# q and k of pairs 4 to 31 loaded by casting transfers of GpSimd, and two more pairs' P turned by TensorE

## The chip, the cores and the metric

The kernel runs on one core of a Trainium2 chip. The metric is the device time of one execution in microseconds (us). TensorE is called PE here, VectorE DVE, ScalarE ACT, GpSimd POOL and SyncE SP; SP only issues transfers.

## The reference

Attention with a forgetting gate, for 8 batches of 8 heads, 576 positions and 64 columns a head, and behind it a gated feed-forward block over the 4608 rows that come out.

```python
scores = (q @ k.T) / sqrt(64)                     # per head, 576 x 576
cum    = cumsum(log(clip(f, 1e-4, 1)), axis=-1)
scores = where(causal, -1e9, scores + cum[..., :, None] - cum[..., None, :])
attn   = exp(scores - max);  attn = attn / (sum(attn) + 1e-9)
x      = (attn @ v) as [4608, 512]                # the heads side by side
g      = x @ w_gate                               # [4608, 1536]
out    = (g * sigmoid(g) * (x @ w_val)) @ w_out   # [4608, 512]
```

## The kernel before

Two neighbouring heads are a *pair*; there are 32 pairs, four to a batch. A pair's query rows are 9 blocks of 64, and the blocks fall into two groups, g = 0 (blocks 0 to 3) and g = 1 (blocks 4 to 8). For each pair the work is:

- **Loads** (`load_pair`). k and q come as fp32, two heads at a time, k in 96 partitions of 6 rows and q in 72 partitions of 8 rows. For pairs 4 to 31 SP issues them into the buffers `kf` and `qf`, two of each. `cb`, the cumulated gate, is loaded with them. Pairs 0 to 3 are loaded in parts (`load_parts`), by SP and ACT.
- **Preparation** (`prepare`, `prepare_parts`). k and q are cast to bf16 (`kb`, `qb`, two buffers each), q with the factor -1/8; for pairs 4 to 31 POOL does this. PE then turns them, by transposes of 64 columns of one head each (`turned`), into the PSUM tile `tx`, and ACT or DVE copies the result to `kt` and `qz` in SBUF, where q's two heads stand in a layout with zeros between them.
- **Scores** (`scores`). PE multiplies `qz` with `kt` into the PSUM tiles `sp`. DVE (L652) subtracts the sum from the gate and takes the row's minimum, and ACT (L672) takes the exponential with the row's sum, into `e` and `eo`.
- **Normalisation** (`normalize`). DVE takes the reciprocals (L690) and POOL scales the rows to bf16 (`pk`, L708). This is the matrix P, in 6 blocks of 128 columns for g = 0 and 19 for g = 1. P has to be turned: for the pairs in `ON_PE` (0 to 7) by PE, a block in two transposes, through PSUM, with evacuations by ACT or DVE (L743); from `JFROM` = 8 on by one transposing DMA of SP for both groups (L721).
- **P times v** (`weighted`, `spread`). PE multiplies, and ACT or DVE writes the result into `xT`, a ring of 2048 rows.

The feed-forward block goes over tiles of 256 or 512 rows of that ring: `gate` multiplies with `wg` and `wv` (PSUM tiles `gv`, L201), ACT takes a tanh, DVE multiplies twice, and `project` multiplies with `wo` and stores. The weights come in pieces by casting transfers of POOL (`weights`, L824 and L828).

All of this is written as a list of operations with allowed engines, estimated costs and priorities. The class `Plan` places them on the engines before the program is made, each at the earliest time by its own estimates, and this fixes each engine's order of instructions. `STARTUP` gives the order of the first loads, `HEAD` that of the first groups of scores, and `NUDGE` small changes of priority for each unit of work (q12: the preparation of pair 12; a12.0: its attention, group 0; f and o: the feed-forward block; v: v's casts). `SLACK` is how long a waiting owner of a shared PSUM pool keeps others out. The engines run their lists in order, and a wait holds up everything behind it on its engine.

Of the kernel before, what the change touches and what calls it, by code (L numbers as in the profile page):

```python
# [8 lines left out]
F32 = mybir.dt.float32  # L9
# [198 lines left out]


def mm(*cols):  # L210
    return sum(max(29, c / 2.4 + 2.5) for c in cols)
# [3 lines left out]
def kernel(  # L215
# [42 lines left out]

    ON_PE = {(p, g) for p in range(8) for g in range(2)}

    JFROM = 8
    TWO = False
    NDIRECT = 0

# [11 lines left out]
    FREE = 8  # L276
    SLACK = 400
    SOON = 8
    BACK = 4
    CBACK = 5  # L280
    STARTUP = "p0 q1 f9 v01 k0 p2 wv2 q0 v04 wv0 wg2 wg0 k2 v00 c3 c1 q3 q2 wv4 v02 p4 c2 v03 c4 wg4 v11 c5 wv8 wg8 v10 v14 p5 v13 wo4 p6 v12 c6 wo0 c7 p7 wo8 c0"
    HEAD = "00 10 20 30 11 01 31 21"


    NUDGE = "a0.0:-6 a1.0:-12.5 a10.0:1 a10.1:1.5 a12.0:-0.5 a13.0:0.5 a13.1:-1 a15.0:-1 a15.1:1 a16.0:-3 a17.0:-2 a17.1:-1.5 a18.0:-0.5 a21.0:-1 a21.1:-1 a22.1:0.5 a25.1:-1 a26.1:-1.5 a27.0:-1.5 a27.1:1 a29.0:2 a30.1:-1 a31.0:0.5 a31.1:0.5 a4.0:2.5 a4.1:2.5 a5.0:-1.5 a5.1:-1 a6.0:0.5 a6.1:1 a7.1:-0.5 a8.0:-1 a9.1:-0.5 f0:4 f1:2 f11:-4 f3:-5 f4:-3.5 f5:-4 f6:-2 f7:1 f8:9.5 f9:0.5 o0:-1 o1:-991 o10:-12.5 o11:3.5 o4:1 o5:-7 o6:-4.5 o8:1 o9:9 q0:-8.5 q1:-12 q10:-1.5 q11:-3 q12:-1.5 q13:-3 q14:-4 q15:-2 q16:-6 q17:1.5 q18:-4 q19:-2 q2:-10 q21:0.5 q24:0.5 q26:2.5 q27:0.5 q29:-2 q3:-9.5 q30:-4 q4:-7 q5:-5 q6:-1 q8:-1 v1:-5.5 v2:-2 v3:3.5 v4:1.5 v5:5.5 v6:0.5 v7:-5"

# [154 lines left out]
    def half(key):  # L441
        return pl.buf(key).bitcast(BF16)


    def load_pair(p):
        b, hp = divmod(p, NPB)
        s = first[p]
        if p < NHALF:
            load_parts(p)
            return  # L450
        for name, src, pr in (("k", k, 0), ("q", q, .1)):
            pl.key((name + "f", p), name + "f")
            loads[name, p] = pl.op({"SP": 620} if p else {"ACT": 620}, lambda e, name=name, src=src: (nc.scalar if e == "ACT" else nc.sync).dma_start(
                out=pl.buf((name + "f", p))[0:ROWS[name][0], :, :],
                in_=src[b, 2 * hp:2 * hp + 2].rearrange("h (p r) d -> p h (r d)", r=ROWS[name][1])),
                (), [(name + "f", p)], (-99 + 3 * p if p < NPB else s - SOON) + pr, dma=1060, pk=68 if name == "k" else 86, after=[sums[p - BACK, 0 if p - BACK >= NPB else 1]] if p >= NPB else [])
        if p >= NSEL:
            pl.key(("cb", p), "cb", p)
            for h in range(2):
                loads["cb", p, h] = pl.op({"SP": 600}, lambda e, h=h: nc.sync.dma_start(  # L460
                    out=pl.buf(("cb", p))[64 * h:64 * h + 64, :],
                    in_=cum_dram[2 * p + h:2 * p + h + 1, :].to_broadcast((64, S))),
                    ["cum_dram"], [("cb", p), (("cb", p), 3)], -98.5 + 3 * p if p < NPB else s - SOON + .2, dma=570, pk=93, after=[sums[p - CBACK, 0 if p - CBACK >= NPB else 1]] if p >= NPB + 1 else [])

    def prepare(p):
# [4 lines left out]
        for name in ("k", "q"):  # L470
            fk, bk = (name + "f", p), (name + "b", p)
            KR, KC = ROWS[name]
            pl.key(bk, name + "b")

            def cast(e, name=name, fk=fk, bk=bk, KR=KR):
                src = pl.buf(fk)[0:KR, :, :].rearrange("p h (r d) -> p r h d", d=D)
                dst = pl.buf(bk)[0:KR, :, :, :]
                if e == "ACT":
                    nc.scalar.activation(dst, src, AF.Copy, scale=-scale if name == "q" else 1.0)
                elif name == "q":  # L480
                    eng[e].tensor_scalar(dst, src, -scale, 1.0, op0=ALU.mult, op1=ALU.mult)  # L481
                else:
                    eng[e].tensor_copy(dst, src)
            engs = {"POOL": 850 if p < 8 else 800 if name == "k" else 1010}
            if p < NPB:
                engs = {"POOL": 850, "ACT": 850, "DVE": 500} if name == "k" else {"POOL": 1050, "ACT": 1050, "DVE": 680}
            o = pl.op(engs, cast, [fk], [bk], s - 1 + (name == "q") * .1)
            o.bias = SPARE if p else {}
            tk = ("tt", name, p)
# [4 lines left out]
            def transpose(e, bk=bk, tk=tk, KR=KR, KC=KC):  # L494
                src = pl.buf(bk).rearrange("p r h d -> p r (h d)")
                for j in range(KC):
                    turned(nc, half(tk)[:, KR * j:KR * j + KR], src[0:KR, j, :], ident[0:KR, 0:KR])
            pl.op({"PE": KC * (KR / 2.4 + 2.5)}, transpose, [bk], [tk, ok], s - 1, lat=200)
            halves = [(0, P, None)] if name == "k" else [(0, 64, 0), (64, 128, 1)]
            for a, z, h in halves:  # L500
                def evac(e, a=a, z=z, h=h, tk=tk, ok=ok, KC=KC):
                    if h is None:
                        src = half(tk)[a:z, 0:S].rearrange("r (j p) -> r p j", j=KC)
                        dst = pl.buf(ok)[a:z, :].rearrange("r (p j) -> r p j", j=KC)
                    else:
                        src = half(tk)[a:z, 0:S].rearrange("r (j i p) -> r i j p", j=R, i=NB)
                        dst = pl.buf(ok)[a:z, :, h, :].rearrange("r i (j p) -> r i j p", j=R)
                    if e == "ACT":
                        nc.scalar.copy(dst, src)  # L509
                    else:  # L510
                        nc.vector.tensor_copy(dst, src)
# [11 lines left out]
    def load_parts(p):  # L523
        b, hp = divmod(p, NPB)
        pl.key(("cb", p), "cb", p)
        for name, x, a, z, r, n in parts(p):
            fk = (name + "f", p, x)
            pl.key(fk, name + "f")
            m = (z - a) // r

            def load(e, u, fk=fk, src=(k if name == "k" else q), a=a, z=z, r=r, m=m):
                h0 = 2 * (hp + u)
                (nc.scalar if e == "ACT" else nc.sync).dma_start(  # L533
                    out=pl.buf(fk)[m * u:m * u + m, :, 0:r * D],
                    in_=src[b, h0:h0 + 2, a:z].rearrange("h (p r) d -> p h (r d)", r=r))
# [12 lines left out]
    def prepare_parts(p):  # L548
        for name, x, a, z, r, n in parts(p):
            fk, bk, tk = (name + "f", p, x), (name + "b", p, x), ("tt", name, p, x)  # L550
            m = (z - a) // r
            pr = min(at[p + u, x == "B"] for u in range(n)) - 1 + (name == "q") * .1
            pl.key(bk, name + "b")
            pl.key(tk, "tx", line="q")

            def cast(e, name=name, fk=fk, bk=bk, r=r, w=m * n):
                src = pl.buf(fk)[0:w, :, 0:r * D].rearrange("p h (r d) -> p r h d", d=D)
                dst = pl.buf(bk)[0:w, 0:r, :, :]
                if e == "ACT":
# [13 lines left out]
            def transpose(e, bk=bk, tk=tk, r=r, w=m * n):  # L573
                src = pl.buf(bk).rearrange("p r h d -> p r (h d)")
                for j in range(r):
                    turned(nc, half(tk)[:, w * j:w * j + w], src[0:w, j, :], ident[0:w, 0:w])
            pl.op({"PE": r * (m * n / 2.4 + 2.5)}, transpose, [bk], [tk] + (oks if x == "A" else []), pr, lat=200, holds=oks)
# [239 lines left out]
    def weights():  # L817
        def piece(engs, fn, reads, writes, *a, **kw):
            loads[writes[0]] = pl.op(engs, fn, reads, writes, *a, **kw)

        cuts = [0, 256, 512, 1024, 1536]
        for a, z in zip(cuts, cuts[1:]):
            for nm, wt, src in (("wg", wg, moe_w_gate), ("wv", wv, moe_w_val)):
                piece({"POOL": 600}, lambda e, wt=wt, src=src, a=a, z=z: nc.gpsimd.dma_start(  # L824
                    out=wt[:, :, a:z], in_=src[:, a:z].rearrange("(ko p) n -> p ko n", p=P)),
                    (), [(nm, n) for n in range(a // P, z // P)], 2 + a / 256, dma=5.1 * (z - a) + 880, pk=20 if z - a == 256 else 42)
        for c in range(0, KF, 4):
# [120 lines left out]
    def unit(o):  # L948
        w = o.writes[0] if isinstance(o.writes[0], tuple) else (o.writes[0],)
        n, *i = w[0] + w[1:] if isinstance(w[0], tuple) else w  # L950
        if n in ("kb", "qb", "kt", "qz", "cm", "kf", "qf", "cb") or n == "tt" and isinstance(i[0], str):
            return f"q{i[0] if n != 'tt' else i[1]}"
# [52 lines left out]
```

## Time and profile before

| | |
|---|---|
| time, median of 3 runs | 414.56 us (410.96, 414.56, 416.29) |
| the profiled execution's own time | 415.21 us |
| its span, in which the profile sees instructions | 413.4 us |
| granted clock of PE in it | 1.0 |
| PE busy | 392.5 us (95%) |
| DVE, ACT, POOL busy | 333.2, 320.5, 271.1 us |
| moved by DMA | 72.16 MB, mean 175 GB/s |

A row of a group names the line, the engine, the operation, what it writes and reads, and how often; behind the bar stand the busy time in us and the mean of one in ns; behind the next bar the engine's idle time before these instructions, and what ended it. A row of the waits reads: engine, tile and line that waited, what it waited for, us in total, times, longest. A row of the timeline starts with the start in us and the length.

### The profile page before, as it was taken

To read this page: it belongs to the slowest core of one execution; us is meant where nothing else is said; L and a number is where in the kernel's file an instruction comes from. 1 tells how busy PE (TensorE), PEld (TensorE's weight loads), DVE (VectorE), ACT (ScalarE), POOL (GpSimd) and SP (SyncE) were. 2 spreads that over 40 slices of the span, in tenths; PEclk is the share of its full clock that TensorE was granted. 3 is DMA by queue.
4 is the path that set the end of the run, shared out by engine and by line. 5 is a ranking of instruction groups with operands and counts; after the bars stand their busy time and mean duration, and the time that the engine had idled before them with its cause. 6 is when DMAs were issued, how large, how long until landed. Compare 5 with 4: busy or idle time off the path is not lost.

```text
span 413.4 us, 15350 instructions
## 1 busy us (share of the span) xinstructions
PE 392.5 (95%) x5848; PEld 269.3 (65%) x5848; DVE 333.2 (81%) x1270; ACT 320.5 (78%) x904; POOL 271.1 (66%) x475
## 2 busy tenths in 40 slices
PE   3988988889999999999999999999999999999996
PEld 2667878777666765567776666665566555568775
DVE  4799987798999789999998999899989952775232
ACT  5799988799999998979998897998899653332221
POOL 7679966699996887799789798878777340000000
PEclk9999999999999999999999999999999999999999
DMA  7999979879799999999999999978996744000211
GB/s 192 190 216 226 216 126 247 163 189 210 184 230 191 229 196 233 241 203 230 224 196 223 234 210 225 239 215 182 201 223 114 149 93 126 2 2 28 79 53 52
DMA packets 144026, 72.16 MB, mean 175 GB/s; under 512 B 117904, under 2 KB 131728, under 8 KB 143952
## 3 DMA queue, kind: packets, MB, share of 16 engines
q1 hardware_dynamic: 137856, 66.21, 74.4%
q0 software_dynamic: 5808, 4.72, 7.9%
q8 instruction: 45, 0.74, 0.8%
q14 instruction: 29, 0.24, 0.2%
q10 hardware_dynamic: 288, 0.26, 0.2%
HBM read 46.65 MB, written 9.58 MB: 136 GB/s over the span
## 4 chain that ended last, share of the span: by engine, by line
PE 81%; DMA 6%; DVE 5%; ACT 3%; issue 2%; POOL 1%; SPq 1%; POOLq 0%; ACTq 0%
PE gv L201 63%; PE sp L201 9%; PE tx L764 4%; PE tx L207 3%; DMA wg<-in_moe_w_gate_dram 3%; DVE t L652 3%; DMA kf<-in_k_dram 2%; PE gv L207 2%; DMA vf<-in_v_dram 1%; ACT eo L672 1%; ACT e L672 1%; SPq L533 1%; POOL vt L811 0%; DVE th L857 0%; ACT kt L509 0%
## 5 line engine op out<-in xcount | busy, mean ns | idle before, releaser
L652 DVE CUSTOM_DVE_ANT_0 t<-sp,cb 128x320 f32<-128x320 f32 (+7 forms) x272 | 121.7, 463 | 9.7 <-PE sp L201 5.1
L708 POOL TENSOR_SCALAR pk<-e,lr 128x512 bf16<-128x512 f32 (+3 forms) x189 | 101.5, 541 | 41.9 <-DVE lr L690 19.7
L201 PE MATMUL gv<-xT,wg 128*64 128x512 bf16 (+2 forms) x1152 | 112.7, 326 | 2.5 <-issue 1.4
L201 PE MATMUL gv<-xT,wv 128*64 128x512 bf16 (+2 forms) x1152 | 112.4, 326 | 0.1
L201 PE MATMUL gv<-wo,hh 128*64 128x512 bf16 (+1 forms) x888 | 106.5, 373 | 0.0
L857 DVE SCALAR_TENSOR_TENSOR th<-th,gv 128x512 f32<-128x512 f32 x108 | 73.9, 684 | 31.3 <-ACT th L855 30.5
L672 ACT ACTIVATE e<-t,tm 128x448 f32<-128x448 f32 (+4 forms) x160 | 88.9, 557 | 5.1 <-DVE tm L652 4.7
L855 ACT ACTIVATE th<-gv 128x512 f32<-128x512 f32 x108 | 64.3, 595 | 35.8 <-PE gv L201 35.2
L201 PE MATMUL sp<-kt,qz 128*64 128x512 bf16 (+7 forms) x640 | 77.9, 294 | 5.3 <-DVE tm L652 3.4
L708 POOL TENSOR_SCALAR pk<-eo,lr 128x256 bf16<-128x256 f32 (+3 forms) x128 | 70.4, 550 | 12.3 <-DVE lr L690 9.0
L201 PEld LDWEIGHTS <-wg 128*64 128x64 bf16 x1152 | 58.8, 110 | 30.0 <-issue 1.6
L201 PEld LDWEIGHTS <-wv 128*64 128x64 bf16 x1152 | 59.8, 110 | 27.4 <-issue 0.4
L860 DVE TENSOR_TENSOR hh<-th,gv 128x512 bf16<-128x512 f32 x108 | 73.7, 684 | 4.8 <-PE gv L201 1.8
L672 ACT ACTIVATE eo<-t,tm 128x256 f32<-128x256 f32 (+3 forms) x128 | 71.3, 558 | 4.3 <-DVE tm L652 3.1
L201 PEld LDWEIGHTS <-hh 128*64 128x64 bf16 x888 | 50.7, 110 | 31.3
L201 PEld LDWEIGHTS <-qz 128*64 128x64 bf16 x640 | 41.7, 113 | 23.0 <-issue 5.9
L884 ACT ACTIVATE ot<-gv 128x512 f32<-128x512 f32 (+1 forms) x34 | 19.9, 584 | 26.2 <-PE gv L201 26.0
L652 DVE DVE_READ_ACCUMULATOR2_ANT tm<- 128x1 f32 x432 | 35.7, 83 | 0.0
L652 DVE CUSTOM_DVE_ANT_0 t<-sp,cm,tm 128x64 f32<-128x64 f32 x128 | 34.4, 277 | 1.2 <-PE sp L201 0.3
L481 POOL TENSOR_SCALAR qb<-qf 72x1024 bf16<-72x1024 f32 x28 | 29.2, 1045 | 2.7 <-DMA qf<-in_q_dram 2.6
L672 ACT ACTIVATION_READ_ACCUMULATOR e<-t,tm 128x1 f32 x160 | 30.8, 193 | 0.0
L764 PE MATMUL tx<-pT,vt 128*64 128x320 bf16 (+4 forms) x448 | 29.6, 263 | 1.2 <-ACT pT L743 0.7
(73 smaller groups left out, 432.3 us busy)
## 6 DMA issues: line engine op xcount, KB each, us to landing
out_dram<-ot SPq DMA_DIRECT2D x35, 256.0 KB
vf<-in_v_dram SPq DMA_DIRECT2D x32, 256.0 KB
cb<-cum_f SPq DMA_DIRECT2D x56, 144.0 KB
kf<-in_k_dram SPq DMA_DIRECT2D x28, 288.0 KB
qf<-in_q_dram SPq DMA_DIRECT2D x28, 288.0 KB
wo<-in_moe_w_out_dram POOLq DMA_DIRECT2D x3, 512.0 KB, 7.0
vf<-in_v_dram SPq DMA_DIRECT2D x8, 128.0 KB
wv<-in_moe_w_val_dram POOLq DMA_DIRECT2D x2, 512.0 KB, 8.8
```

The lines of the kernel that those rows point to most:

```text
L201: nc.tensor.matmul(out[c, :], lhsT[:, c], rhs, **kw)
L207: nc.tensor.transpose(out[c, :], src[:, c], ident)
L481: eng[e].tensor_scalar(dst, src, -scale, 1.0, op0=ALU.mult, op1=ALU.mult)
L533: (nc.scalar if e == "ACT" else nc.sync).dma_start(out=pl.buf(fk)[m * u:m * u + m, :, 0:r * D], in_=src[b, h0:h0 + 2, a:z].rearrange("h (p ...
L652: nc.vector.tensor_tensor_reduce(out=pl.buf(tk)[:, a:z], in0=pl.buf(sk)[:, o:o + z - a], in1=pl.buf(("cm", p))[:, i, :] if own else pl.buf ...
L672: nc.scalar.activation(pl.buf(ek)[:, :L], pl.buf(tk)[:, :L], AF.Exp, bias=pl.buf(("tm", p, g))[:, 0, i:i + 1], scale=-1.0, accum_out=pl.bu ...
L708: eng[e].tensor_scalar(dst, src, r, 1.0, op0=ALU.mult, op1=ALU.mult)
L764: nc.tensor.matmul(xo[r, 0:QB * n], vt[:, c, 2 * hp + h, :], pT[:, a:a + n, 64 * h:64 * h + 64], start=(c == 0), stop=(c == nch - 1))
L855: pl.op({"ACT": 487}, lambda e, u=u: nc.scalar.activation(pl.buf(("th", t, u)), pl.buf(("wg", t, u)), AF.Tanh, scale=0.5), [("wg", t, u)], ...
L857: pl.op({"DVE": 605}, lambda e, u=u: nc.vector.scalar_tensor_tensor(pl.buf(("th", t, u)), pl.buf(("th", t, u)), 1.0, pl.buf(("wg", t, u)), ...
L860: pl.op({"DVE": 605}, lambda e, u=u: nc.vector.tensor_mul(pl.buf(("hh", t, u)), pl.buf(("th", t, u)), pl.buf(("wv", t, u))), [("u", t, u), ...
L884: nc.scalar.mul(pl.buf(ok)[:, a:z], pl.buf(bk)[:, 0:z - a], 0.5)
```

## The change

For pairs 4 to 31, POOL issues the loads of q and k as transfers that cast from fp32 to bf16, straight into `qb` and `kb`, of which there are now three each (`NQB`). The casts of these pairs by POOL and the buffers `qf` are gone, `kf` is left for pairs 0 to 3, whose bf16 rows now have buffers of their own (`kc`, `qc`) and whose q comes by way of a `cm` buffer. The two heads of a row stand one behind the other in the bf16 buffers instead of side by side, which `turned_rows` takes into account; number and shape of the transposes stay. The factor -1/8 of q moves from the cast into the evacuation of `qz`. `ON_PE` takes in pairs 8 and 9, and `JFROM` is 10. The rule that keeps casting transfers of POOL apart at the start now holds for weights alone (`o.dma > 1100`). `SLACK`, `STARTUP` and `NUDGE` are new, so the whole order of the instructions is. By the instruction lists, two of the 16 additions of the mask (`cm`, L607) go from POOL to DVE.

```diff
+def turned_rows(nc, out, src, ident):
+    for h in range(2):
+        nc.tensor.transpose(out[64 * h:64 * h + 64, :], src[:, h, :], ident)
...
-    ON_PE = {(p, g) for p in range(8) for g in range(2)}
-    JFROM = 8
+    ON_PE = {(p, g) for p in range(10) for g in range(2)}
+    JFROM = 10
+    NQB = 3
...
-    SLACK = 400
+    SLACK = 100
-    STARTUP = "p0 q1 f9 v01 k0 p2 wv2 q0 v04 wv0 wg2 wg0 k2 v00 c3 c1 q3 q2 wv4 v02 p4 c2 v03 c4 wg4 v11 c5 wv8 wg8 ..."
+    STARTUP = "f9 p0 q1 k0 v01 p2 wv2 q0 wg2 v04 wv0 v00 wg0 q3 c1 c3 k2 wv4 p4 q2 v02 c2 c4 wg4 v03 wg8 v11 wv8 c0 p5 ..."
-    NUDGE = "a0.0:-6 a1.0:-12.5 a10.0:1 ..."
+    NUDGE = "a0.0:0.5 a0.1:-3 a1.0:-85.5 ..."
...
-    bufs("qf", [P, 2, ROWS["q"][1] * D], F32, 2)
-    bufs("kf", [P, 2, ROWS["k"][1] * D], F32, 2)
-    bufs("qb", [P, ROWS["q"][1], 2, D], BF16, 2)
-    bufs("kb", [P, ROWS["k"][1], 2, D], BF16, 2)
+    bufs("kf", [P, 2, 5 * D], F32, 2)
+    bufs("qc", [P, 2, 4 * D], BF16, 2)
+    bufs("kc", [P, 2, 5 * D], BF16, 2)
+    bufs("qb", [P, 2, ROWS["q"][1] * D], BF16, NQB)
+    bufs("kb", [P, 2, ROWS["k"][1] * D], BF16, NQB)
...
-            loads[name, p] = pl.op({"SP": 620} if p else {"ACT": 620}, lambda e, name=name, src=src: (nc.scalar if e == "ACT" else nc.sync).dma_start(
-                out=pl.buf((name + "f", p))[0:ROWS[name][0], :, :],
-                in_=src[b, 2 * hp:2 * hp + 2].rearrange("h (p r) d -> p h (r d)", r=ROWS[name][1])),
+            loads[name, p] = pl.op({"POOL": 560}, lambda e, src=src, bk=bk, w=ROWS[name]: nc.gpsimd.dma_start(
+                out=pl.buf(bk)[0:w[0], :, :], in_=src[b, 2 * hp:2 * hp + 2].rearrange("h (p r) d -> p h (r d)", r=w[1])),
...
-            def cast(e, name=name, fk=fk, bk=bk, KR=KR):
-                ...
-            engs = {"POOL": 850 if p < 8 else 800 if name == "k" else 1010}
-            ...
-            o = pl.op(engs, cast, [fk], [bk], s - 1 + (name == "q") * .1)
...
-                src = pl.buf(bk).rearrange("p r h d -> p r (h d)")
                 for j in range(KC):
-                    turned(nc, half(tk)[:, KR * j:KR * j + KR], src[0:KR, j, :], ident[0:KR, 0:KR])
+                    turned_rows(nc, half(tk)[:, KR * j:KR * j + KR], pl.buf(bk)[0:KR, :, D * j:D * j + D], ident[0:KR, 0:KR])
...
-                    if e == "ACT":
+                    if h is not None and e == "ACT":
+                        nc.scalar.mul(dst, src, -scale)
+                    elif h is not None:
+                        nc.vector.tensor_scalar(dst, src, -scale, None, op0=ALU.mult)
+                    elif e == "ACT":
                         nc.scalar.copy(dst, src)
...
-        if "POOL" in o.engs:
+        if "POOL" in o.engs and o.dma > 1100:
             o.after.append(line[n - BEHIND])
-            o.after += [x for x in line[:n] if "POOL" in x.engs][:-1][-1:]
+            o.after += [x for x in line[:n] if "POOL" in x.engs and x.dma > 1100][:-1][-1:]
```

More of the change, by code (lines that the diff above doesn't have):

```diff
@@ L442, in half, with rows @@
         return pl.buf(key).bitcast(BF16)
+    def rows(key):
+        x = pl.buf(key)
+        return x if key[0] == "kf" else x.rearrange("p i c -> p (i c)")[:, 0:8 * D].rearrange("p (h x) -> p h x", h=2)
     def load_pair(p):
@@ L470, in prepare @@
         for name in ("k", "q"):
-            fk, bk = (name + "f", p), (name + "b", p)
+            bk = (name + "b", p)
             KR, KC = ROWS[name]
-            pl.key(bk, name + "b")
-            def cast(e, name=name, fk=fk, bk=bk, KR=KR):
-                src = pl.buf(fk)[0:KR, :, :].rearrange("p h (r d) -> p r h d", d=D)
-                dst = pl.buf(bk)[0:KR, :, :, :]
-                if e == "ACT":
[L479 to L483, printed above, removed]
-            engs = {"POOL": 850 if p < 8 else 800 if name == "k" else 1010}
-            if p < NPB:
-                engs = {"POOL": 850, "ACT": 850, "DVE": 500} if name == "k" else {"POOL": 1050, "ACT": 1050, "DVE": 680}
-            o = pl.op(engs, cast, [fk], [bk], s - 1 + (name == "q") * .1)
-            o.bias = SPARE if p else {}
             tk = ("tt", name, p)
@@ L533, in load @@
                 (nc.scalar if e == "ACT" else nc.sync).dma_start(
-                    out=pl.buf(fk)[m * u:m * u + m, :, 0:r * D],
+                    out=rows(fk)[m * u:m * u + m, :, 0:r * D],
                     in_=src[b, h0:h0 + 2, a:z].rearrange("h (p r) d -> p h (r d)", r=r))
@@ L825, in weights @@
                     out=wt[:, :, a:z], in_=src[:, a:z].rearrange("(ko p) n -> p ko n", p=P)),
-                    (), [(nm, n) for n in range(a // P, z // P)], 2 + a / 256, dma=5.1 * (z - a) + 880, pk=20 if z - a == 256 else 42)
+                    (), [(nm, n) for n in range(a // P, z // P)], 2 + a / 256, dma=5.1 * (z - a) + 880, pk={256: 20, 512: 42, 1024: 84}[z - a])
         for c in range(0, KF, 4):
```

28 lines of the change are left out of this document (14 added, 14 removed).

## The prediction

> **What bounds the kernel now.** I read the page first, then the busy time of each engine by stage (start us:end us, length, then busy us and instructions per engine, granted clock, share of the DMA engines, GB/s), with the stages cut where TensorE's (PE's) share changes, and then what PE waited for.
>
> ```profile
> span 413.4 us, 15350 instructions
> PE 392.5 (95%) x5848; PEld 269.3 (65%) x5848; DVE 333.2 (81%) x1270; ACT 320.5 (78%) x904; POOL 271.1 (66%) x475
> ```
> ```profile
> 0.00:15.00 15.00, 7.83 (x68) 5.35 (x68) 7.63 (x26) 9.67 (x24) 11.00 (x41) 1.00 0.81 187
> 15.00:40.00 25.00, 21.21 (x343) 16.20 (x344) 23.20 (x97) 22.82 (x73) 20.22 (x38) 1.00 1.15 216
> 40.00:70.00 30.00, 26.82 (x622) 24.83 (x623) 25.80 (x80) 25.99 (x66) 24.34 (x40) 1.00 1.01 200
> 70.00:105.00 35.00, 32.05 (x656) 26.21 (x654) 29.57 (x113) 31.34 (x89) 27.03 (x47) 1.00 0.85 193
> 105.00:330.00 225.00, 224.46 (x3002) 143.71 (x3000) 207.12 (x888) 203.41 (x599) 183.32 (x301) 1.00 1.01 207
> 330.00:409.50 79.50, 79.50 (x1164) 52.72 (x1160) 39.87 (x72) 26.50 (x55) 5.18 (x10) 1.00 0.19 54
> ```
> ```profile
> PE tx L207 <- POOL kb L483: 0.4, 1, 0.4
> PE tx L207 <- POOL qb L481: 0.2, 1, 0.2
> ```
>
> The last fence is the whole list of PE's waits from 105 us on: 0.6 us. From 105 to 409.5 us PE has work all the time (224.46 of 225 us, then 79.50 of 79.50), and from 330 us on GpSimd (POOL) is nearly done while PE still has 79.5 us to go. So behind 105 us a faster POOL, DVE, ACT or DMA is worth nothing, PE work that is added costs its full length, and a late load costs whatever PE then stands still. Ahead of 105 us PE idles 7.17 + 3.79 + 3.18 + 2.95 = 17.1 us. Of that, 9.9 us lie behind 15 us. There alone is something to gain.
>
> **The change, part by part.** *P of pairs 8 and 9 by TensorE.* A pair has 6 + 19 blocks of 128 columns, each two transposes of 64 rows: 100 new PE instructions. Their price, and that of their evacuations and of the DMA transposes that go:
>
> ```profile
> 63.80 0.45 PE gv L207 x16
> L743 ACT COPY pT<-gv 128x1024 bf16<-128x1024 bf16 x7 | 7.0, 1002 | 0.1
> L743 DVE COPY pT<-gv 128x768 bf16<-128x768 bf16 x5 | 2.8, 550 | 0.0
> L743 DVE COPY pT<-gv 128x384 bf16<-128x384 bf16 x5 | 1.8, 352 | 0.0
> L721 SPq DMA_TRANSPOSE pT<-pk x24: 3754/4632/6587, 106.2 to 337.2; - x24
> ```
>
> Sixteen take 0.45 us in the chain, 28 ns each, so 100 take **2.8 us**. They fall at about 100 us and later, where PE is full, so I count all of it. Their evacuations, by the changed kernel's instruction lists, are 4 x 1.00 us on ACT and 2 x 0.55 + 2 x 0.35 = 1.8 us on DVE; ACT has 225 - 203.41 = 21.6 us idle in the long stage and DVE 17.9 us, which hides them (4 to 6 us if that cover were gone). Two DMA transposes of 4.6 us leave SP's queue; nothing waited long for them, so I take 0. The 24 transposes start between 106.2 and 337.2 us, so a pair takes 231 / 23 = 10.0 us there.
>
> *The casts that go, the issues that come.* POOL loses 28 casts of q and 28 of k and issues 56 casting transfers instead:
>
> ```profile
> L481 POOL TENSOR_SCALAR qb<-qf 72x1024 bf16<-72x1024 f32 x28 | 29.2, 1045 | 2.7 <-DMA qf<-in_q_dram 2.6
> L483 POOL CAST kb<-kf 96x768 bf16<-96x768 f32 x28 | 23.1, 825 | 0.9 <-DMA kf<-in_k_dram 0.8
> L824 POOL DMA_DIRECT2D wv<-in_moe_w_val_dram x4: 751/798/962, 9.9 to 40.2; - x4
> L453 SPq DMA_DIRECT2D kf<-in_k_dram x28: 313/470/2204, 25.2 to 305.4; - x28
> wv<-in_moe_w_val_dram POOLq DMA_DIRECT2D x2, 512.0 KB, 8.8
> wv<-in_moe_w_val_dram POOLq DMA_DIRECT2D x2, 256.0 KB, 7.0
> q0 software_dynamic: 5808, 4.72, 7.9%
> q1 hardware_dynamic: 137856, 66.21, 74.4%
> ```
>
> Removed: 29.2 + 23.1 = 52.3 us. Added: POOL's issue of a weight piece, the nearest row, took 0.75 to 0.96 us; SP's issue of the very same k took 0.31 at least. I take 0.8, since engine and cast are those of the weight rows: 56 x 0.8 = 45 us. POOL ends some 7 us lighter (bounds: 35 lighter to 1 lighter), and two more mask additions move from POOL to DVE. On the path this is **0**: POOL has slack behind 105 us, and the next thing late would be PE. The waits move, too. A transfer now waits on POOL for its kb or qb buffer, which comes free when PE has turned q and k of three pairs before, and the normalisations (pk) of the current pair stand behind it; for them wait the P transposes. In the changed order the issue stands about two pairs ahead of PE's use, some 20 us, against 7.0 to 8.8 us from issue to landing. So I take 0 here as well, and the rival below takes the other end. For the DMA engines, q0 moved 4.72 MB (counted after the cast) in 7.9% of the span, 6.9 us per MB; 8.26 MB of q and k make 57 us. The plain queue moved its 66.21 MB in 74.4%, 4.6 us per MB; the same loads as 16.5 MB of fp32 make 77 us by its mean. No rise, 0.
>
> [...]
>
> *The scale of q, now in the evacuation of qz.*
>
> ```profile
> L509 ACT COPY qz<-tx 64x576 bf16<-64x576 bf16 x40 | 25.3, 632 | 3.7 <-PE tx L207 1.7 <-DVE qz L511 1.5
> L511 DVE COPY qz<-tx 64x576 bf16<-64x576 bf16 x16 | 7.2, 453 | 3.1 <-PE tx L207 2.6 <-ACT qz L509 0.3
> L886 DVE TENSOR_SCALAR ot<-gv 128x512 f32<-128x512 f32 x3 | 2.1, 691 | 0.8 <-PE gv L201 0.8
> ```
>
> The instruction count stays. A scaled DVE evacuation is bounded by the 453 ns of the copy and the 691 ns of a scaled fp32 one: 0 to 16 x 0.24 = 3.8 us of DVE, inside its 17.9 us of idle time. 0 on the path. The transposes of q and k keep their number and shape: 0.
>
> *The start.* f is now SP's first load instead of its fourth:
>
> ```profile
> 0.74 0.76 SPq L533 DMA_DIRECT2D kf<-in_k_dram  x1
> 3.14 0.50 SPq L398 DMA_DIRECT2D t<-in_f_dram  x1
> 6.97 0.45 DVE L400 TENSOR_SCALAR t<-t 64x576 f32<-64x576 f32 x1 [2.98 <-DMA t<-in_f_dram]
> 8.17 1.35 DVE L403 TENSOR_TENSOR_SCAN t<-tiny,t 64x576 f32<-64x576 f32 x1 [0.75 <-ACT t L402]
> 9.72 2.93 PE L425 MATMUL gv<-t,one 64*128 64x256 f32 x6
> 12.57 0.64 PE L207 MATMUL tx<-ident,kb 128*64 128x128 bf16 x8
> 13.00 0.48 PE L207 MATMUL tx<-ident,qb 80*64 80x80 bf16 x8
> 12.29 0.42 DVE L652 CUSTOM_DVE_ANT_0 t<-sp,cb 128x256 f32<-128x256 f32 x1
> ```
>
> Issued at 0.74 as SP's first was, f lands 2.4 us earlier, and the scan ends at about 7.1 instead of 9.5. But in the new order three selecting matmuls (2.93 us) and eight transposes (0.43 us from their start to the next) stand ahead of the first scores, which formerly ran ahead of them: 7.1 + 0.2 + 2.93 + 0.43 = 10.7, and with the scores and an evacuation DVE begins at about 11.3 rather than 12.29. So **-1.0 us**, between -2.4 (the whole lead) and 0.
>
> *The rest of the new order.* Up to the end of pair 7 the scores have the same PE work ahead of them in both lists; in between, the new one has fewer gate matmuls ahead of the attention of pairs 5 to 7. That can go either way, from -9.9 us (all the idle time of 15 to 105 us) to the 4.1 us of the weights below. I take 0, because the same loads, pools and engines fill this stretch.
>
> **Sum.** 413.4 + 2.8 - 1.0 = 415.2 us of span. The profiled run took 415.21, 1.8 more than its span, and stands 0.65 above the median of 414.56. So 414.56 + 1.8 = **416.4 us**: no change that a measurement of this kernel can tell, for which about 2% are needed.
>
> **The rivals.** *Weights late* (a loss inside 2%). In q0 four new transfers, k and q of pairs 4 and 5, 576 KB after the cast, go ahead of the last pieces of the gate weights. 512 KB landed 1.8 us later than 256 KB, so 576 KB are 4.1 us. The last piece is on the chain already:
>
> ```profile
> 42.69 12.02 DMA wg<-in_moe_w_gate_dram
> ```
>
> If all of it comes out on PE: 416.4 + 4.1 = 420.5 us. Against it: PE has other work at that place.
>
> *POOL blocked* (slower). In 105 to 330 us POOL was busy 183.32 us, of which 21 + 21 casts were 39.3. 144.0 us remain, so 225 - 144.0 = 81 us are left for some 42 issues and their waits: up to 1.93 us each costs nothing. Behind that point pk is late, then the P transposes, then PE's next attention matmul, and since PE's order is fixed, no gate work steps in: 4.2 us for every 0.1 us. At 2.2 us, an issue of 0.8 and 1.4 of wait for the buffer, it is 0.27 x 42 = 11.4 us: **427.8 us**. For it: the wait for PE is new on POOL, and any stall feeds back. Against it: POOL's slack of 42 us and the order's lead. [...]
>
> *A better filled start* (faster). Much of the idle time behind 15 us has causes that an order can remove, such as these waits of PE:
>
> ```profile
> PE tx L207 <- ACT kb L560: 4.6, 1, 4.6
> PE sp L201 <- DVE tm L652: 3.4, 9, 1.0
> ```
>
> (The first of them is the very start.) With the whole lead of f and all 9.9 us gone it is 414.56 + 2.8 - 2.4 - 9.9 = **405.1 us**. For it: ACT loses casts at the start, and attention comes further forward. Against it: DVE and ACT were busy 23.20 and 22.82 of 25 us there.
>
> *The change does nothing it says*: the casts of 28 pairs do go, so only its effect can be nil; that is the forecast without its two terms, 414.6, and the same class.
>
> **How the numbers follow.** The forecast has 0.36 and weights late 0.08: within 2% (406.3 to 422.9) together 0.44. POOL blocked has 0.34, since the new wait is shown by no row and one average wait of 1.4 us suffices. The better start has 0.22, since it needs nearly all of its room. Likeliest is 416.4 us; its own range is 410 to 421. The range goes down to 404.5, about the full better start, and up to 430, just behind POOL blocked at 2.2 us; outside I leave a little on either side.
>
> **What would show it.** Right: PE waits of under 2 us behind 105 us, 500 transposes of pk, POOL issues of about 0.8 us, DVE's first scores at about 11.3 us, and PE's idle time of 15 to 105 us near 10 us. Wrong: in the list of waits "PE <- POOL pk" or "PE <- DMA kb", a busy share of PE below 99% in 105 to 330 us (slower); or idle time of 15 to 105 us under 3 us (faster).

## The result and the profile after

The changed kernel takes **433.01 us** (median of 4 runs, 428.34 to 438.55); the kernel before, beside it, 414.46. The ratio is 1.042, with a 95% interval of 1.030 to 1.055: slower by over 2%, where 416.4 us and no change were forecast, and above the forecast's range (404.5 to 430). The medians here and below are of all runs; the ratios leave out a few that were slower at a lower clock, of the changed kernel the one of 438.55 us. The profiled execution took 434.43 us, with a span of 432.7.

The head of the page, and the busy time by stage in the columns of the prediction:

```profile
span 432.7 us, 15500 instructions
PE 399.2 (92%) x5948; PEld 271.0 (63%) x5948; DVE 338.5 (78%) x1284; ACT 320.1 (74%) x899; POOL 257.2 (59%) x474
```
```profile
0.00:15.00 15.00, 7.06 (x56) 4.36 (x56) 7.83 (x24) 8.44 (x20) 10.33 (x40) 1.00 0.78 180
15.00:40.00 25.00, 21.17 (x382) 16.54 (x379) 22.09 (x94) 23.48 (x79) 21.00 (x38) 0.93 1.13 206
40.00:70.00 30.00, 27.92 (x665) 26.54 (x666) 29.64 (x101) 27.34 (x73) 26.56 (x46) 1.00 0.87 152
70.00:105.00 35.00, 34.90 (x719) 28.36 (x716) 32.51 (x127) 32.59 (x96) 30.25 (x58) 1.00 0.92 179
105.00:330.00 225.00, 208.96 (x2772) 130.80 (x2770) 187.69 (x795) 187.03 (x541) 152.99 (x268) 0.98 0.94 163
330.00:409.50 79.50, 79.50 (x930) 48.82 (x928) 51.64 (x138) 35.10 (x87) 16.08 (x29) 1.00 0.31 71
```

TensorE (PE) was idle for 17.1 us ahead of 105 us before, and now for 7.94 + 3.83 + 2.08 + 0.10 = 13.95 us: 3.1 less. From 105 to 330 us it was idle for 0.5 us before, and now for 16.0. That is the loss. The list of PE's waits from 105 us on, whole (total, times, longest):

```profile
PE tx L212 <- DMA qb<-in_q_dram: 6.1, 3, 3.4
PE tx L212 <- DMA kb<-in_k_dram: 5.5, 3, 4.0
PE tx L762 <- DMA pT<-pk: 4.2, 2, 3.0
```

Three kinds of transfer land late, 15.8 us together: the new casting loads of q and of k, and the transposing transfers of P, which were there before and for which PE never waited. No line of this list names POOL. POOL itself did stand still for late transposing transfers, 12.2 us in three waits of pk (1.0 us in the kernel before).

The span is 19.3 us longer. PE's idle time is 12.6 of it (432.7 - 399.2 = 33.5, against 20.9): -3.1 ahead of 105 us, +15.5 from 105 to 330 us, and 0.2 in the tail. The other 6.7 us are busy time (399.2 against 392.5): some 2.8 are the 100 new transposes by the prediction's estimate, and a lower clock, which the next rows show, is large enough for the rest. They cut the trace into slices of 3.41 us, which is how long the clock stayed low each time, around stretches in which PE had little work, with the granted clock third from the end:

```profile
22.30:25.72 3.42, 1.72 (x32) 1.12 (x33) 2.73 (x16) 3.17 (x17) 3.30 (x9) 1.00 1.30 226
25.72:29.13 3.41, 3.41 (x46) 2.64 (x46) 3.41 (x12) 3.37 (x10) 3.32 (x7) 0.50 0.57 93
```
```profile
138.36:141.77 3.41, 0.20 (x10) 0.20 (x12) 0.00 (x0) 2.56 (x10) 0.00 (x0) 1.00 1.15 161
141.77:145.18 3.41, 3.41 (x34) 1.76 (x30) 1.61 (x4) 0.00 (x0) 2.37 (x5) 0.50 1.22 230
281.72:285.13 3.41, 1.20 (x14) 0.47 (x8) 3.21 (x11) 2.29 (x6) 0.25 (x1) 1.00 1.16 84
285.13:288.54 3.41, 3.22 (x30) 1.76 (x32) 0.78 (x2) 1.29 (x2) 1.64 (x4) 0.50 1.13 271
302.20:305.61 3.41, 1.51 (x24) 0.70 (x20) 3.30 (x15) 1.24 (x4) 3.17 (x6) 1.00 1.38 111
305.61:309.02 3.41, 1.88 (x32) 1.07 (x32) 0.00 (x0) 1.35 (x3) 2.50 (x6) 1.00 1.91 111
309.02:312.44 3.42, 0.37 (x6) 0.07 (x4) 0.69 (x1) 1.46 (x5) 0.00 (x0) 1.00 0.96 147
312.44:315.85 3.41, 3.41 (x28) 2.01 (x30) 1.70 (x9) 1.04 (x4) 1.22 (x2) 0.50 1.31 224
```

After the slices in which PE was busy for 1.72, 0.20, 1.20 and 0.37 us, the clock of the next slice is 0.50. In one of these, eight matmuls of 128x512 took 1.70 us from their start (285.81 us) to that of the next work, and just behind it 0.86 (288.89 us). So I estimate that a half-clock slice costs at most half its length, 1.7 us: 5.1 us for the three behind 105 us, so a long wait can be paid more than once, and 1.7 for the one at the start. The kernel before has a clock of 1.00 in every stage up to 409.5 us.

**One wait, read through.** First what POOL and SP issued around 273 us, then what PE did (start, us, line, idle time before it and its releaser):

```profile
273.24 0.70 POOL L466 DMA_DIRECT2D kb<-in_k_dram  x1
273.94 0.69 POOL L466 DMA_DIRECT2D qb<-in_q_dram  x1
```
```profile
273.32 9.93 SPq L719 DMA_TRANSPOSE pT<-pk  x1
```
```profile
285.32 0.69 PE L212 MATMUL tx<-ident,qb 72*64 72x72 bf16 x16 [2.40 <-DMA qb<-in_q_dram]
```
```profile
320.38 0.39 PE L201 MATMUL sp<-kt,qz 128*64 128x256 bf16 x6
```

A pair has one issue of qb, 16 turning matmuls of q and 20 matmuls of scores (28 issues for pairs 4 to 31, 448 and 640 matmuls in all), so the n-th of each belongs together. This is pair 29. The transposing transfers, all of them:

```profile
L719 SPq DMA_TRANSPOSE pT<-pk x22: 3666/4422/9928, 122.2 to 355.4; - x22
```

Its q was issued at 273.94 us, within a microsecond of a transposing transfer whose issue held SP for 9.93 us (4.42 is the middle of 22), and it landed 11.3 us later. It is not the only one: six of the 56 casting loads took over 9.5 us to land, and each was issued at most 3.2 us behind one of the three transposing transfers that took longest themselves (issued at 129.07, 273.32 and 296.96 us, landed 13.6, 13.4 and 15.4 us later). PE had reached the turning of q 2.4 us earlier and stood still. But the scores that need it begin at 320.38 us, 35 us on.

So it is for all pairs from 12 on. From the issue of k to its scores there are 21.1 us at least, 31.6 in the middle, 47.1 at most. But from the issue to PE's *turning* there are 4.3, 8.2 and 17.7 (for q 5.9, 9.3 and 23.0). POOL's issues and their landings (duration ns min/median/max, first and last start, then us to landing):

```profile
L466 POOL DMA_DIRECT2D kb<-in_k_dram x28: 662/690/717, 29.9 to 298.2; - x28
L466 POOL DMA_DIRECT2D qb<-in_q_dram x28: 681/691/744, 31.2 to 298.9; - x28
DMA to landing us min/median/max: 3.4/5.8/13.4
```

The planner's own line says why the turnings stand there. It puts each operation at the earliest time it can have, and takes a load of POOL as landed after 2.85 us, its 1.06 us on a free wire, and 0.50, which is 4.4 us:

```python
head, tail = (2850, 500) if q else ...      # q: issued by POOL
...
o.end = wire[q] + tail                      # the turning may stand here in PE's order
```

### The profile page after: what moved, and what is told of

It is laid out like the page before. It is cut to its first block, busy times and chain, and to the rows that moved or that the text cites. A ratio compares the mean times of both kernels' runs of the same rounds, so it can differ in the third digit from the quotient of the medians.

```text
span 432.7 us, 15500 instructions
## 1 busy us (share of the span) xinstructions
PE 399.2 (92%) x5948; PEld 271.0 (63%) x5948; DVE 338.5 (78%) x1284; ACT 320.1 (74%) x899; POOL 257.2 (59%) x474
## 3 DMA queue, kind: packets, MB, share of 16 engines
q0 software_dynamic: 17456, 12.99, 23.4%
## 4 chain that ended last, share of the span: by engine, by line
PE 66%; DMA 18%; POOL 6%; DVE 4%; issue 2%; SPq 2%; ACT 0%; POOLq 0%; DVEq 0%; ACTq 0%
PE gv L201 51%; PE sp L201 7%; DMA kb<-in_k_dram 6%; DMA pT<-pk 6%; POOL pk L706 4%; PE tx L762 4%; PE tx L212 3%; DMA qb<-in_q_dram 3%; PE gv L207 2%; DMA vf<-in_v_dram 2%; DVE t L650 2%; SPq L532 1%; DMA cb<-cum_f 1%; DMA cm<-in_q_dram 1%; DVE th L855 1%
## 5 line engine op out<-in xcount | busy, mean ns | idle before, releaser
L706 POOL TENSOR_SCALAR pk<-e,lr 128x128 bf16<-128x128 f32 (+3 forms) x191 | 102.5, 540 | 43.9 <-DVE lr L688 15.4
L201 PE MATMUL gv<-xT,wg 128*64 128x512 bf16 (+2 forms) x1152 | 113.9, 329 | 0.0
L670 ACT ACTIVATE e<-t,tm 128x64 f32<-128x64 f32 (+4 forms) x160 | 88.7, 557 | 7.4 <-DVE tm L650 6.5
L201 PE MATMUL sp<-kt,qz 128*64 128x512 bf16 (+7 forms) x640 | 76.8, 295 | 5.3 <-DVE tm L650 4.9
L670 ACT ACTIVATE eo<-t,tm 128x384 f32<-128x384 f32 (+3 forms) x128 | 71.3, 558 | 8.7 <-POOL pk L706 4.3
L706 POOL TENSOR_SCALAR pk<-eo,lr 128x384 bf16<-128x384 f32 (+2 forms) x127 | 67.8, 534 | 11.9 <-DMA pT<-pk 4.9
L201 PEld LDWEIGHTS <-hh 128*64 128x64 bf16 x888 | 49.7, 111 | 32.6 <-issue 1.5
L762 PEld LDWEIGHTS <-vt 128*64 128x64 bf16 x448 | 24.3, 112 | 11.8 <-DMA pT<-pk 5.2
L504 ACT ACTIVATE qz<-tx 64x576 bf16<-64x576 bf16 x40 | 25.7, 641 | 8.0 <-PE tx L212 7.7
```

The costliest lines, as they stand in the source:

```text
L201: nc.tensor.matmul(out[c, :], lhsT[:, c], rhs, **kw)
L504: nc.scalar.mul(dst, src, -scale)
L670: nc.scalar.activation(pl.buf(ek)[:, :L], pl.buf(tk)[:, :L], AF.Exp, bias=pl.buf(("tm", p, g))[:, 0, i:i + 1], scale=-1.0, accum_out=pl.bu ...
L706: eng[e].tensor_scalar(dst, src, r, 1.0, op0=ALU.mult, op1=ALU.mult)
L762: nc.tensor.matmul(xo[r, 0:QB * n], vt[:, c, 2 * hp + h, :], pT[:, a:a + n, 64 * h:64 * h + 64], start=(c == 0), stop=(c == nch - 1))
```

## The experiments

The theory after the result (A): the loss is late landings, because the turnings and the products with P stand in PE's order at about the shortest landing (4.4 us in the plan, 3.4 at least in the trace), and casting and transposing transfers delay each other. Rivals: the order of work is worse by itself; POOL's issues block; the P transposes cost more than their sum.

**e_early**: PE's, ACT's, DVE's and SP's orders fixed, the casting transfers of pairs 12 to 31 earlier in POOL's.

```diff
-        for o in pl.order():
+        made = pl.order()
+        ...
+                when[o.n] = min(o.start, max(o.start - 8000, gone.end))   # gone: the turning that frees the buffer
+        for o in sorted(made, key=lambda o: (when[o.n], o.n)):
```

> The changed kernel with PE, ACT, DVE and SP in the same order; only in POOL's list the transfers of q and k of pairs 12 to 31 stand up to 8 us of the plan earlier, behind the turning that frees their buffer. Late transfers (the issue stands about 5 us ahead of PE's need and lands in 5 to 13 us): the 11.6 us of PE's waits for kb and qb fall under 2 us, two of the three clock drops behind 105 us go with them (1.7 us each), so 433.0 - 9.6 - 3.4 = 420 us. Rival, the new order as such or the extra P transposes: the waits only move to other causes, 430 to 436 us. Rival, POOL blocked by the waits of the issues: POOL's normalisations get later, waits of PE for pT grow, over 433 us.

Measured: 427.97 us, ratio 1.032 (1.028 to 1.036). The row of the long stage and the first of PE's waits from 105 us on:

```profile
105.00:330.00 225.00, 214.94 (x2852) 146.32 (x2854) 198.87 (x821) 191.29 (x558) 154.49 (x270) 0.98 0.94 166
```
```profile
PE tx L762 <- DMA pT<-pk: 7.1, 2, 3.8
```

The waits for q and k are gone, but the wait for P grew from 4.2 to 7.1, and two half-clock slices behind 105 us are left. The time is 5.0 us lower, which is not clear of noise, since the changed kernel's ratio is known only to 1.030 to 1.055. The expected 420 was not reached: only the q and k part was cured.

**e_copy**: the transposing transfers of pairs 10 to 31 become plain copies of the same bytes; P of these pairs stays unturned.

```diff
-    nc.sync.dma_start_transpose(out=both["pT"][...], in_=both["pk"][...].rearrange("p s k -> p (s k)"))
+    nc.sync.dma_start(out=both["pT"][...], in_=both["pk"][...])
```

> The changed kernel in the same order, but the 22 transposing transfers of P are plain copies of the same bytes (P is not turned, which leaves that part of the computation out). If the transposing transfers are what makes q and k land late: no landing of kb or qb over 7 us, PE waits for them under 2 us, the 4.2 us for pT gone, about 417 us. If the casting transfers are late by themselves or by the load of plain bytes: landings of 8 to 13 us stay, PE's waits for kb and qb stay near 11 us, 428 us or more.

Measured: 419.93 us, ratio 1.013 (1.009 to 1.016), 13.1 us less than the changed kernel. The long stage and all of PE's waits from 105 us on:

```profile
105.00:330.00 225.00, 219.75 (x2916) 141.80 (x2912) 200.69 (x845) 197.20 (x571) 162.37 (x281) 0.98 0.66 170
```
```profile
PE tx L212 <- DMA qb<-in_q_dram: 2.7, 3, 1.1
PE tx L212 <- DMA kb<-in_k_dram: 2.6, 3, 1.6
```

The waits for P go, as they must; but those for q and k halve too, though nothing of these loads was touched, and the longest landing falls from 13.4 to 9.6 us (waits under 2 us and 7 us were expected). So the transposing transfers delay the casting ones. (The share of the DMA engines, next to last in the row, falls from 0.94 to 0.66: plain copies of the same bytes also hold the engines for less time.)

**e_tiny**, the other way round: the casting transfers of pairs 12 to 31 carry 8 partitions, so the scores of these pairs are computed partly from older rows.

```diff
-    out=pl.buf(bk)[0:w[0], :, :], in_=src[...].rearrange("h (p r) d -> p h (r d)", r=w[1])
+    out=pl.buf(bk)[0:n, :, :],    in_=src[...].rearrange("h (p r) d -> p h (r d)", r=w[1])[0:n]    # n = 8 from pair 12 on
```

> The changed kernel in its own order, but each casting transfer of q and k of pairs 12 to 31 carries only 8 of its 72 or 96 partitions (24 or 32 KB instead of 288 KB read); the rest of these buffers keeps rows of earlier pairs, so scores of these pairs are computed from stale data. The issues on POOL, the transposing transfers of P and every order stay. Theory A (casting and transposing transfers delay each other at the DMA engines): q and k land within 2.5 to 4.5 us, none of them is waited for, and the transposing transfers, which the changed kernel landed after 5.6 us at least, 7.8 in the middle and 15.4 at most, come down to a longest landing of 9 us or less, so that the wait for pT (4.2 us) goes too: 414 to 418 us. Rival B (the transposing transfers are late by the order alone, not by the casting ones): the waits for kb and qb go (11.6 us), the wait for pT of 4 to 7 us and a clock drop or two remain, as they did with the earlier issues (427.97 us): 419 to 425 us.

Measured: 414.60 us, ratio 1.0015 (0.998 to 1.005): as fast as the kernel before. The long stage, all of PE's waits from 105 us on, and the landing of the transposing transfers, first in this kernel and then in the changed one:

```profile
105.00:330.00 225.00, 224.02 (x2994) 152.72 (x2992) 209.24 (x883) 201.80 (x587) 162.39 (x290) 1.00 0.73 150
```
```profile
PE gv L201 <- DVE th L855: 0.5, 1, 0.5
PE tx L762 <- DMA pT<-pk: 0.4, 1, 0.4
```
```profile
DMA to landing us min/median/max: 5.6/6.6/8.5
```
```profile
DMA to landing us min/median/max: 5.6/7.8/15.4
```

Same orders, same 56 issues on POOL (0.55 to 0.63 us each in the middle, after 0.69), only fewer bytes in the casting transfers: the longest landing of P falls from 15.4 to 8.5 us and the whole loss is gone. The shortened loads themselves landed after 4.3 us in the middle and 6.6 at most; 2.5 to 4.5 were expected. Rival B of its expectation, that P is late by the order alone, falls.

**e_early_copy**: both edits at once.

> Two of the parts at once, in the changed kernel's own order: the casting transfers of pairs 12 to 31 up to 8 us earlier in POOL's order, and the joint transposing transfers of P of pairs 10 to 31 replaced by plain copies of the same bytes between the same buffers, so that P of these pairs stays unturned (that part of the computation is left out). Nothing else is moved. Theory A (the whole loss is late landings, of q, k and of P, and the clock drops that the waits bring): no DMA wait of TensorE over 1 us and no clock drop between 105 us and the tail, TensorE's busy time over 222 us of the 225 in 105 to 330, and a time of 411 to 416 us, below the 419.9 us of the plain copies alone. Rival B (the new order of work costs by itself, as the re-planned order of the P-only kernel did with its 425.1 us): waits on DVE or ACT take the place of the transfers' and the time stays at 419 to 424 us. Rival C (earlier casting transfers only delay others): the landings of cb or vf become the waits, and the time is 418 us or more.

Measured: 414.97 us, ratio 0.999 (0.996 to 1.002). The long stage, and all of PE's waits from 105 us on:

```profile
105.00:330.00 225.00, 222.93 (x2996) 156.59 (x2992) 208.92 (x879) 201.53 (x589) 165.57 (x288) 1.00 0.67 171
```
```profile
PE gv L201 <- DVE hh L858: 1.2, 1, 1.2
PE gv L207 <- POOL pk L706: 0.4, 1, 0.4
PE sp L201 <- DVE tm L650: 0.3, 1, 0.3
```

By the ratios, which are taken against the kernel before in the same set of runs, the two parts are worth some 1% and 3% alone and 4.3% together; within the noise of the changed kernel they add up. Without late landings, the new order, the 100 transposes and the 56 issues come out where the kernel before was. No half-clock slice is left behind 105 us. That the order itself is worse (rival B) falls, and so does every theory in which the 56 issues, here of full length, cost by themselves.

**e_p_only**, the kernel before with P of pairs 8 and 9 on PE, and **e_qk_only**, the changed kernel without that, each placed anew by the planner (`ON_PE` and `JFROM`: 8 becomes 10, and 10 becomes 8).

> The kernel before with pairs 8 and 9 turned by TensorE and nothing else, planned anew from its constants. If 100 transposes at 28 ns are all it costs: 414.5 + 2.8 = 417 us, PE waits behind 105 us under 2 us. If this part or any new plan carries the loss: 425 us or more.

> The casting transfers alone: P of pairs 8 and 9 by transposing DMA as before, the rest as in the changed kernel, planned anew from its constants. If the transfers carry the loss: PE waits of some 8 to 16 us for kb, qb and pT behind 105 us, 426 to 434 us. If the two pairs' P turned by TensorE carry it: 412 to 417 us.

Measured: 425.06 us, ratio 1.025 (1.020 to 1.029), and 441.29 us, ratio 1.061 (1.056 to 1.066). The largest of PE's waits from 105 us on, of the one and of the other:

```profile
PE sp L201 <- DVE tm L652: 3.7, 5, 1.0
```
```profile
PE tx L212 <- DMA qb<-in_q_dram: 6.7, 4, 2.4
PE sp L201 <- DVE tm L650: 5.5, 6, 2.5
PE tx L212 <- DMA kb<-in_k_dram: 3.3, 2, 2.4
```

Both keep the values of `NUDGE` that belong to another set of operations, and waits for DVE appear that neither kernel has. They do not tell the parts apart: in the first there is no casting transfer of q or k, and it still loses 10 us. To tell parts apart, one has to be changed at a fixed order, as above.

**e_p_twice**: the 100 transposes of P of pairs 8 and 9 twice, in the changed kernel's order.

```diff
+    for _ in range(2 if p in (8, 9) else 1):
         for x in range(a, z):
             turned(nc, bank()[...], pl.buf(kk)[:, x, :], ident)
```

> The changed kernel in its own order, with the 100 transposes of P of pairs 8 and 9 on TensorE done twice over into the same banks (the result is the same, nothing is left out). Theory A (these transposes lie in idle time of TensorE between 40 and 105 us): within 1 us of the changed kernel's 433.0 us, and the idle time between 15 and 105 us, 6.0 us in the changed kernel, falls by about as much as the transposes add there. Rival B (TensorE is full there, the prediction's term): 2.8 us more, 435.8 us, with the idle time unchanged. Later landings may move by a few tenths of a per cent either way, so the reading goes by the windows up to 105 us first and by the time second.

Measured: 438.71 us (432.55 to 446.20), ratio 1.049 (1.036 to 1.061), which cannot be told from the changed kernel's 1.030 to 1.055. The same product with v in the changed kernel and here (its profiled execution was the longest of its runs, so only the part ahead of 140 us is read):

```profile
133.87 0.88 PE L762 MATMUL tx<-pT,vt 128*64 128x320 bf16 x14
```
```profile
137.21 0.88 PE L763 MATMUL tx<-pT,vt 128*64 128x320 bf16 x14
```

Ahead of all long waits the work stands 3.3 us later: PE is full at that place. Behind it the late landings differ, so the total decides between neither theory. The price was therefore measured where nothing lands late:

**e_clean** (e_early_copy once more), **e_clean_p0** (84 of the 100 transposes left out) and **e_clean_p2** (all 100 done twice):

```diff
-    for x in range(a, z):
+    for x in range(a, a + 1 if p in (8, 9) else z):          # e_clean_p0; the copy out likewise
```

> The kernel of e_early_copy once more (casting transfers of pairs 12 to 31 earlier, P of pairs 10 to 31 copied and not turned, which is left out of the computation), as the base for the next two, in which nothing lands late: 414 to 416 us, no DMA wait of TensorE behind 105 us.

> e_clean, and of the 25 blocks of P of pair 8 and of pair 9 only the first of each bank, 4 a pair, is turned and copied out; 84 of the 100 new transposes are left out, and 21 blocks of each of these two pairs' P keep rows of earlier pairs. Theory A (the prediction's term, 28 ns each on a full TensorE): 84 x 0.028 = 2.4 us below e_clean. Rival B (they fill idle time of 15 to 105 us): within 0.8 us of e_clean, and the idle time of 15 to 105 us, 6.2 us in e_early_copy, grows by 2 us.

> e_clean, and the 100 transposes of P of pairs 8 and 9 done twice over. Theory A: 2.8 to 3.3 us above e_clean, as the same doubling put the changed kernel's work at 134 us back by 3.3 us. Rival B (the delay there is made up behind it): within 1 us of e_clean.

Measured: 416.22 us (ratio 1.006, 1.002 to 1.009), 413.68 us (1.002, 1.000 to 1.005) and 418.04 us (1.011, 1.005 to 1.018). The transposes of pk in these kernels are 500, 416 and 600. In e_clean no wait for a transfer is left behind 105 us; it is the kernel that stood at 0.999 as e_early_copy, so two sets of runs can differ by 0.7%, and the three are compared with each other.

84 fewer are worth 2.5 us, 30 ns each, and PE's idle time of 15 to 105 us does not take their place (8.2 us in e_clean, 8.0 in e_clean_p0), so rival B falls there. 100 more cost 1.8 us, less than the 2.8 expected; with four runs, from 416.96 to 419.44 us, this does not by itself exclude the 1 us of rival B. The term holds by the first of the two.

**m_late**: landings told to the planner as 3.5 us later for the casting transfers and 2.5 us later for the transposing ones, with values of `NUDGE` for that. **m_late_qk**: the same, with P of pairs 8 and 9 by the transposing transfer.

```diff
-    o.end = wire[q] + tail
+    o.end = wire[q] + tail + (3500 if q and o.dma == 1060 else 2500 if o.ring else 0)
```

> The changed kernel with the landing times that the kernel's own planner assumes raised by 3.5 us for the casting transfers of q and k and by 2.5 us for the transposing ones, and new values of NUDGE for that; nothing else differs, and the output is the reference's. So PE's turnings of q and k move back in PE's order, to behind the landings that the trace shows, instead of the issues forward. Theory A (the loss is where the turnings stand in PE's order): from issue to turning 8 us or more in nearly all pairs, where the changed kernel had 4.3 us at least and 8.2 in the middle, DMA waits behind 105 us under 3 us together, no clock drop there, and 413 to 419 us. Rival B (any re-planned order costs by itself, as the P-only kernel's 425.1 us): waits on other engines take their place, 420 to 428 us. Rival C (the landings grow wherever the turnings stand, since the transfers collide): DMA waits of 8 us or more stay, 425 to 433 us.

> As m_late, but with P of pairs 8 and 9 turned by the transposing transfer as in the kernel before, and values of NUDGE of its own. Theory A (the 100 transposes of P cost their 2.8 to 3.3 us on PE, and the rest of the change gains about 3 us at the start once nothing lands late): 1 to 4 us below m_late, 410 to 416 us, so as fast as the kernel before or a little faster. Rival B (P of pairs 8 and 9 by transfers is late itself, as it was in the q-and-k-only kernel with its 441.3 us): waits for pT of 3 us or more between 95 and 140 us and a time at or above m_late's.

Measured: 421.68 us, ratio 1.015 (1.004 to 1.025), and 421.31 us, ratio 1.011 (1.001 to 1.020). The long stage of the first, and all of PE's waits from 105 us on:

```profile
105.00:330.00 225.00, 221.91 (x2980) 155.68 (x2978) 209.51 (x871) 198.26 (x580) 166.61 (x291) 0.99 0.95 175
```
```profile
PE tx L762 <- DMA pT<-pk: 2.3, 1, 2.3
PE sp L201 <- DVE tm L650: 0.6, 1, 0.6
```

From issue to turning there are now 7.2 us at least and 10.6 in the middle (4.3 and 8.2 before), no wait for q or k is left, and 11.3 of the 18 us come back with the computation whole. It is above the 419 us of theory A: one wait for P and one half-clock slice remain, and PE is busy for longer than in e_early_copy (its row first, then that of m_late), which I did not resolve:

```profile
PE 393.0 (95%) x5948; PEld 290.5 (70%) x5948; DVE 339.7 (82%) x1284; ACT 318.3 (77%) x899; POOL 257.0 (62%) x474
```
```profile
PE 398.2 (95%) x5948; PEld 295.4 (71%) x5948; DVE 342.6 (82%) x1281; ACT 322.0 (77%) x905; POOL 255.3 (61%) x471
```

The 1 to 4 us that the second was to gain over the first did not show (their intervals overlap), so I have no version faster than the kernel before.

## Why the prediction was wrong

**The step that failed** is the lead of the casting transfers. "In the changed order the issue stands about two pairs ahead of PE's use, some 20 us, against 7.0 to 8.8 us from issue to landing. So I take 0 here as well." I measured the lead to the scores, and it is there: 21.1 us at least. But PE's first use is the turning, 8.2 us behind the issue in the middle and 4.3 at least, and PE takes its list in order, so it stood still at the turning (2.40 us for pair 29) however early that stands for the scores (35 us on). The term was not 0 but about 17 us with all that follows it (433.0 against 414.97 and 416.22 without late landings).

**The second half of that step**, 7.0 to 8.8 us to landing, took medians of weight pieces. The middle of q and k was better, 5.8 us, but a wait is made by the longest, 13.4. The transfers' load as a mean was judged rightly, "No rise": the share of the DMA engines in the long stage was 1.01 before and 0.94 after. What the mean hid is two kinds of transfer in flight together. q0 moves the casting transfers (12.99 MB, 4.72 in the kernel before) and q1 the transposing ones among others (from 105 us on it had 102173 packets, and 34261 in e_copy); with either kind made harmless the other's longest landing fell from 13.4 to 9.6 us and from 15.4 to 8.5. Both edits also lighten the engines' load (share 0.66 and 0.73), so whether it is the meeting of the two kinds or the load at that moment that delays them stays open; the kernel before had a share of 1.01 and PE waited for no transfer behind 105 us. How the two kinds share an engine was not shown.

**A cost that no term had**: the half clock behind a wait (0.50 in three slices of 3.41 us), at most 5.1 us behind 105 us by the estimate above.

**Right**: the P transposes (2.8 us, 28 ns each, forecast; 30 ns for each one left out, 18 for each one added). The issue on POOL, 0.8 forecast and 0.69 measured, 0.74 at most. The scale of q: the evacuations took 641 ns on ACT and 452 on DVE, after 632 and 453.

```profile
L504 ACT ACTIVATE qz<-tx 64x576 bf16<-64x576 bf16 x40 | 25.7, 641 | 8.0 <-PE tx L212 7.7
L506 DVE TENSOR_SCALAR qz<-tx 64x576 bf16<-64x576 bf16 x16 | 7.2, 452 | 0.5 <-ACT qz L504 0.3
```

The sum, too, comes out without its failed step: 1.8 us above the kernel before were forecast, and the kernel without late landings stands 0.1% below it in one comparison and 0.6% above it in the other. That is partly luck, since the terms of the start and of the rest of the order came out otherwise and about made up for each other.

**The start** came out otherwise. f first was to bring DVE's first scores to 11.3 us instead of 12.29; they began at 13.33, 1.0 us later than before and not 1.0 earlier, although the scan of f ended at 7.5 us, about where it was forecast (7.1):

```profile
13.33 0.42 DVE L650 CUSTOM_DVE_ANT_0 t<-sp,cb 128x256 f32<-128x256 f32 x1 [1.16 <-PE sp L201]
```
```profile
7.94 0.48 PE L212 MATMUL tx<-ident,qc 80*64 80x80 bf16 x8 [7.94 <-POOL qc L561]
```
```profile
4.61 0.64 PE L207 MATMUL tx<-ident,kb 128*64 128x128 bf16 x8 [4.61 <-ACT kb L560]
```

PE's first transposes waited for a cast on POOL until 7.94 us, 3.3 later than those of the kernel before (the last row); that this used up f's lead is the likely reading, which no run tested. On the other side, the idle time of 15 to 105 us, which I left at 10 us, fell to 6.0 (8.2 in the profile of e_clean). The rival of the better filled start had its place right, but at most two fifths of its size.

**The rival "POOL blocked"** has nearly the time, 427.8 us, but not the cause: POOL is lighter by 13.9 us, and the list of PE's waits from 105 us on does not name it. The stall that "feeds back" is there in part: POOL stood 12.2 us for late P. But in e_tiny, with the same order and as many issues, that wait is 2.9 us and the loss is gone. The signs named for a wrong forecast did appear: "PE <- DMA kb", and a busy share of PE of 92.9% (208.96 of 225 us) in 105 to 330 us.

## What to carry to other kernels

Measure a load's lead to the first instruction that waits for it on an in-order engine, not to the work that needs its data: a preparatory step that is placed as early as the data can land turns late landings into stalls (11.6 us in six waits here). Take the longest landing with everything else in flight, and place the use that far behind the issue (m_late won back 11.3 us that way); keeping loads and transposing transfers apart in time was not tried. And take one part of such a change out at a fixed order: a part that is planned anew brings a loss of its own (10 us here, of which some 3 were the part).

## What the runs showed of the hardware

- The granted clock drops to 0.50 for 3.41 us at a time. In the changed kernel this starts, up to 409.5 us, at 25.72, 141.77, 285.13 and 312.44 us, each time behind a slice with 0.20 to 1.72 us of work of TensorE. The steps between these starts are 34, 42 and 8 times 3.413 us (286.72 us in 84 parts), and in e_early the two starts behind 105 us, 194.35 and 259.20 us, are 19 times that apart. So I take it, without a run that tests it, that what happens within a fixed slice counts, not the length of a wait: the wait of 3.43 us that ended at 307.14 us lay across two slices (1.51 and 1.88 us busy, rows above) and brought no drop; one of 2.40 us did.
- The busy time of a slice alone does not give the border: one of 1.72 us was followed by a drop, one of 1.51 us was not. In e_copy (from 295.55 us) and in e_p_only (from 315.34 us) a second half-clock slice followed the first, with 2.61 and 2.04 us busy in that first. And at the start of the changed kernel, where TensorE's first work stands at 7.94 us, the clock was 1.00 up to 15 us. What decides was not shown.
- A transposing transfer that runs beside casting ones can hold SP's issue for 9.93 us (4.42 in the middle), and land after 15.4 us; with the casting ones shortened (e_tiny) the longest are 5.19 and 8.5 us. Casting loads of q and k are not the only thing that lengthens the hold: in e_p_only, which has none, it reaches 7.91 us.
- The same order of work can differ by 2 us in the idle time of 15 to 105 us from one execution to another (6.2 in e_early_copy, 8.2 in e_clean).
